# A new order for 1680 operations: linear attention fused with a squared-ReLU FFN on one core

## The chip, the core and the metric

The kernel runs on one core of a Trainium2 chip. Its engines are TensorE (PE, matmuls; PEld is its weight load), VectorE (DVE), ScalarE (ACT), GpSimd (POOL) and SyncE (SP); each works through its own instructions in order and waits on semaphores for the others. Matmuls write into PSUM, which has eight banks of 512 fp32 numbers in each of 128 partitions. The metric is the time of one execution in microseconds (us), as the median of several runs; a profile shows one execution.

## The reference

The input is q, k, v of 8 batches, 8 heads, 576 positions and 64 channels, a projection w_phi of 64 x 128, and the weights of an FFN. What is computed, cut to what matters:

```python
def phi(x):
    proj = np.einsum('bhsd,df->bhsf', x, w_phi)
    proj = proj - np.max(np.abs(proj), axis=-1, keepdims=True)
    return np.concatenate([np.exp(proj), np.exp(-proj)], axis=-1)
q_p, k_p = phi(q), phi(k)
kv  = np.einsum('bhsf,bhsd->bhfd', k_p, v)
z   = np.sum(k_p, axis=2)
num = np.einsum('bhsf,bhfd->bhsd', q_p, kv)
den = np.einsum('bhsf,bhf->bhs', q_p, z)[..., None] + 1e-06
x   = (num / den).transpose(0, 2, 1, 3).reshape(4608, 512)
h   = np.maximum(x @ w_in, 0.0)          # w_in: 512 x 2048
out = (h * h) @ w_out                    # w_out: 2048 x 512
```

The matmuls take bf16 operands; inputs and output are fp32.

## The kernel before, in words

The program first writes down a plan: 1680 operations, each with its engine, a function that issues its instructions, and the tags that it reads and writes. They are numbered in the order of writing, and the numbers are used as names below ("projection 42"). Then it issues them in the order of a table. Nothing decides at run time; each engine's instructions stand in exactly that order.

**Attention, by batch.** POOL loads k, q and v (L249, L257, L269, L278) into two buffers each. Of the first two batches PE transposes k and q (L320), and DVE or ACT copies the result to SBUF (kT, qT; L193 is the copy on DVE, L195 that on ACT). From batch 2 on SP does it with a DMA transpose (L331). A projection of k (Pk: L347, and in halves L379 for the first group) fills two banks; *three* operations then read it: the largest magnitude on DVE (mk, L405, in halves L386), and exp of plus and minus the projection on ACT (kp and kn, L411, in halves L394). The maximum isn't needed by the exps: its own exp (va, L420) is multiplied into v (L428) instead. PE sums kp and kn against v (L450, L462) and the result kv is copied to SBUF. For q the first batches use L491/L498 and turned projections Fq (L569, exps L584); from batch 3 on projections Pq with maxima L531 and exps qf (L544), which SP turns by DMA (qpn). NA (L648) and NB are the two parts of the numerator, with a DVE scaling SA (L660) between; then a reciprocal (L670) and xo, the quotient (L674), which closes the numerator's banks. There are three xo buffers. SP turns xo into xT by DMA (L708); for the first batch PE does it.

**FFN, by chunks of 512 tokens.** F1 (L788; L799, L813, L827 for the first chunk) multiplies four 128 x 512 blocks into one bank; relu moves it to hr, on ACT (L765) or on DVE (L767), and frees the bank; DVE squares it (L774). F2 (L882) sums sixteen blocks into one bank in four operations; a copy takes it to ot, and SP stores it. There are four hr and four ot buffers.

All the program between batches is one interleaved stream: while PE works on the FFN of one chunk, DVE and ACT prepare the next batch's attention.

**What sets the order.** Five tables at the end: ORDER (the order of issue), BASES (a bank for each use of PSUM), STATES (for operations that two engines can do, which does it), GATES (for each load of batches 2 to 7, the operation behind which POOL issues it) and FILL (dummy matmuls on a tile `warm` ahead of a PE operation, L961). PSUM is one tile, and what touches the same bank from two engines is kept in the order of the program by semaphores, readers too. POOL keeps at most eight loads outstanding. The lines which use the tables:

```python
    def arrange(self):
        for op in self.ops:
            if op.alt is not None and STATES[op.group] == "1":
                op.eng, op.occ, op.lat = op.alt
        for g, b in zip(self.banks, BASES):
            g.base = int(b)
        return [self.ops[i] for i in ORDER]
...
        if now[0].seq in GATES:
            dep(i, plan.ops[GATES[now[0].seq]].ins, mybir.DependencyClass.Sync)
...
    for op in plan.arrange():
        if op.seq in FILL:
...
            bank, n = FILL[op.seq]
            for _ in range(n):
                pin(nc.tensor.matmul(out=psum[:, bank, :P], lhsT=warm, rhs=warm, start=True, stop=True))
```

Of the kernel before, what the change touches and what calls it, by code (L numbers as in the profile page):

```python
# [108 lines left out]
def kernel(  # L109
# [945 lines left out]
)  # L1055
STATES = (
    '0100000001011000100001110011010100000000100011100100110000001010000000010110000100000000001000000100'
    '0100101101000000011010011011010000010100000111010001000100000000010110000100001101000000000000111111'
    '101000110110110110111110101110000'
)  # L1060
GATES = {
# [46 lines left out]
```

## Time and profile before

| | |
|---|---|
| median of 3 runs | 344.05 us (343.82 to 346.07) |
| span of the profiled execution | 344.8 us, 0.75 above the median |
| PE busy | 335.5 us, 97% of the span |
| DVE busy | 264.2 us, 77% |
| ACT busy | 225.4 us, 65% |
| POOL busy | 95.5 us, 28% |
| moved by DMA | 51.51 MB, 149 GB/s on average |

"Busy" is the time in which an engine executes; a matmul that waits for a semaphore isn't busy. The shares are means over stages of different kinds: a startup of some 26 us in which the first two batches are prepared and no FFN runs yet, a middle in which FFN and attention are interleaved, and a stretch from about 250 us in which only the FFN of the last chunks is left. Rows of groups give the number of instructions behind x, then busy time and mean nanoseconds of one, then the idle time ahead of them with what ended it. Rows of waits give the total, how often, and the longest.

### The profile page before, as it was taken

How to read it: one execution, taken by the hardware profiler on the slowest of the kernel's cores; microseconds unless marked ns; L12 is line 12 of the kernel's file. 1: busy time of each engine (PE TensorE's matmuls, PEld its weight loads, DVE VectorE, ACT ScalarE, POOL GpSimd, SP SyncE). 2: the span in 40 equal slices, each digit the busy share in tenths (PEclk: the TensorE clock that was granted, in tenths of full speed). 3: DMA queues.
4: the chain of work that ended last, by engine and by line, in shares of the span. 5: the costliest groups of instructions: out<-in, count | busy, mean ns of one | idle time of the engine just before them, and what ended most of it. 6: DMA issues, size and time to landing. Idle time of an engine off the chain costs nothing.

```text
span 344.8 us, 8417 instructions
## 1 busy us (share of the span) xinstructions
PE 335.5 (97%) x3389; PEld 188.3 (55%) x3389; DVE 264.2 (77%) x485; ACT 225.4 (65%) x393; POOL 95.5 (28%) x143
## 2 busy tenths in 40 slices
PE   8999999799999999999999999999999999999995
PEld 7679776444654555545545554565555444444443
DVE  4999999699877987788898999687876635757510
ACT  4999996489898898476887797798475503210031
POOL 8670671681730390104604051240000000000000
PEclk9999999999999999999999999999999999999999
DMA  9999999999999999999999999999864821101024
GB/s 139 179 206 202 199 132 157 153 118 205 170 175 172 227 165 185 195 182 183 171 207 172 199 164 195 188 154 168 196 125 96 157 62 38 63 0 61 32 68 115
DMA packets 142935, 51.51 MB, mean 149 GB/s; under 512 B 111472, under 2 KB 138416, under 8 KB 142896
## 3 DMA queue, kind: packets, MB, share of 16 engines
q1 hardware_dynamic: 97488, 32.35, 50.7%
q0 software_dynamic: 44960, 18.23, 46.7%
q8 instruction: 26, 0.43, 0.5%
q10 hardware_dynamic: 448, 0.39, 0.4%
q14 instruction: 13, 0.11, 0.1%
HBM read 36.73 MB, written 9.44 MB: 134 GB/s over the span
## 4 chain that ended last, share of the span: by engine, by line
PE 87%; DMA 6%; DVE 3%; ACT 1%; POOL 1%; issue 0%; POOLq 0%; DVEq 0%; SPq 0%
PE psum L788 32%; PE psum L882 31%; PE psum L648 5%; PE psum L462 5%; PE psum L347 5%; DMA xT<-xo 4%; DMA qpn<-qf 3%; PE psum L827 2%; PE psum L569 1%; DVE mk L405 1%; PE psum L813 1%; PE psum L799 1%; PE psum L846 1%; PE psum L450 1%; PE psum L320 1%; PE psum L961 1%
## 5 line engine op out<-in xcount | busy, mean ns | idle before, releaser
L882 PE MATMUL psum<-wout,h 128*128 128x512 bf16 x560 | 132.6, 380 | 0.0
L788 PE MATMUL psum<-xT,win 128*128 128x512 bf16 x448 | 106.1, 379 | 0.6 <-DMA xT<-xo 0.6
L765 ACT ACTIVATE hr<-psum 128x512 bf16<-128x512 f32 x98 | 57.1, 600 | 57.7 <-PE psum L788 50.2
L882 PEld LDWEIGHTS <-h 128*128 128x128 bf16 x560 | 51.1, 98 | 56.5 <-issue 0.3
L788 PEld LDWEIGHTS <-win 128*128 128x128 bf16 x512 | 46.7, 97 | 51.9 <-DMA xT<-xo 1.4
L774 DVE TENSOR_TENSOR h<-hr 128x512 bf16<-128x512 bf16 x144 | 56.0, 415 | 18.7 <-ACT hr L765 18.2
L544 ACT ACTIVATE qf<-psum 128x1024 bf16<-128x1024 f32 (+1 forms) x50 | 46.1, 939 | 5.5 <-PE psum L347 2.0
L405 DVE TENSOR_REDUCE mk<-psum 128x8 f32<-128x1024 f32 (+1 forms) x38 | 42.4, 1120 | 3.9 <-PE psum L347 2.0
L411 ACT ACTIVATE kn<-psum 128x1024 bf16<-128x1024 f32 (+1 forms) x38 | 35.7, 948 | 8.2 <-PE psum L347 4.7
L411 ACT ACTIVATE kp<-psum 128x1024 bf16<-128x1024 f32 (+1 forms) x38 | 35.8, 951 | 4.8 <-PE psum L347 4.0
L648 PEld LDWEIGHTS <-qpn 128*128 128x128 bf16 x624 | 27.5, 97 | 16.6 <-issue 3.1
L767 DVE TENSOR_SCALAR hr<-psum 128x512 bf16<-128x512 f32 x46 | 31.1, 684 | 5.7 <-PE psum L788 4.2
L660 DVE TENSOR_TENSOR psum<-psum,en 128x520 f32<-128x520 f32 (+1 forms) x39 | 27.2, 702 | 10.3 <-PE psum L648 6.1
L648 PE MATMUL psum<-kv,qpn 128*128 128x65 bf16 x624 | 30.6, 193 | 2.5 <-DVE xo L674 2.4
L269 POOL DMA_DIRECT2D xq<-in_q_dram x24 | 17.3, 727 | 55.2 <-DVE h L774 14.3
L531 DVE TENSOR_REDUCE mq<-psum 128x8 f32<-128x1024 f32 (+1 forms) x25 | 27.8, 1112 | 3.3 <-PE psum L347 2.5
L674 DVE TENSOR_TENSOR xo<-psum,rden 128x512 bf16<-128x512 f32 (+1 forms) x39 | 26.4, 684 | 3.7 <-DMA xT<-xo 3.2
L249 POOL DMA_DIRECT2D xk<-in_k_dram x27 | 20.0, 744 | 32.5 <-ACT en L508 16.0
L584 ACT ACTIVATE qpn<-psum 128x1024 bf16<-128x1024 f32 (+1 forms) x30 | 26.8, 955 | 2.5 <-PE psum L569 2.2
L195 ACT ACTIVATE ot<-psum 128x512 f32<-128x512 f32 x24 | 14.4, 598 | 20.3 <-PE psum L882 20.1
L428 DVE TENSOR_TENSOR va<-xv,va 128x1280 bf16<-128x1280 bf16 (+2 forms) x34 | 23.4, 714 | 0.8 <-ACT va L420 0.8
L249 POOL DMA_DIRECT2D xv<-in_v_dram x27 | 19.9, 744 | 14.7 <-PE psum L788 11.1
(79 smaller groups left out, 348.9 us busy)
## 6 DMA issues: line engine op xcount, KB each, us to landing
out_dram<-ot SPq DMA_DIRECT2D x32, 256.0 KB, 2.9
xk<-in_k_dram POOLq DMA_DIRECT2D x25, 128.0 KB, 5.6
xq<-in_q_dram POOLq DMA_DIRECT2D x24, 128.0 KB, 4.5
xv<-in_v_dram POOLq DMA_DIRECT2D x24, 128.0 KB, 5.0
win<-in_moe_w_in_dram POOLq DMA_DIRECT2D x4, 512.0 KB, 9.8
wout<-in_moe_w_out_dram POOLq DMA_DIRECT2D x4, 512.0 KB, 15.1
xq<-in_q_dram POOLq DMA_DIRECT2D x4, 256.0 KB, 6.4
out_dram<-ot SPq DMA_DIRECT2D x6, 128.0 KB, 2.3
```

Of the source, the lines that this page charges most:

```text
L249: pin(nc.gpsimd.dma_start(out=x[:, m0 + a * 512 : m0 + z * 512].rearrange("p (h x) -> p h x", x=4 * D), in_=src[b][2 * a : 2 * z, 0:512, : ...
L405: pin(nc.vector.tensor_reduce(out=mk_view(g), in_=ps2(pj)[:, :, : n * Fd].rearrange("p e (i f) -> p e i f", f=Fd), axis=AX.X, op=ALU.max, ...
L411: pin(nc.scalar.activation(out=dst[slot][:, :, :n, :].rearrange("p e i f -> p e (i f)"), in_=ps2(pj)[:, :, : n * Fd], func=ACT.Exp, scale= ...
L531: pin(nc.vector.tensor_reduce(out=mqb[:, c, :, :n], in_=ps2(pj)[:, :, : n * Fd].rearrange("p e (i f) -> p e i f", f=Fd), axis=AX.X, op=ALU ...
L544: pin(nc.scalar.activation(out=o, in_=i_, func=ACT.Exp, scale=sgn))
L648: pin(nc.tensor.matmul(out=o[:, u // 4, u % 4 * D1 : (u % 4 + 1) * D1], lhsT=qpn[slot][:, sg * half + u * m : sg * half + u * m + P], rhs= ...
L660: pin(nc.vector.tensor_tensor(out=o, in0=o, in1=enb[:m, c, :].rearrange("t (b h) -> t b h", b=2).to_broadcast([m, 2, 4, D1]), op=ALU.mult))
L765: pin(nc.scalar.activation(out=hr[sl], in_=ps1(g), func=ACT.Relu))
L767: pin(nc.vector.tensor_scalar(out=hr[sl], in0=ps1(g), scalar1=0.0, scalar2=None, op0=ALU.max))
L774: pin(nc.vector.tensor_tensor(out=dst, in0=i_, in1=i_, op=ALU.mult))
L788: pin(nc.tensor.matmul(out=o, lhsT=win[mc // 4][:, kc, mc % 4 * P : (mc % 4 + 1) * P], rhs=x, start=(kc == 0), stop=(kc == KC - 1)))
L882: pin(nc.tensor.matmul(out=ps1(g), lhsT=h2[c % 2][mc // 4][:, mc % 4, tt * P : (tt + 1) * P], rhs=wout[mc // 4][:, mc % 4, :], start=(mc = ...
```

## The change

All five tables get other contents; the 1680 operations, their functions and the data stay the same. The core of the diff:

```diff
 ORDER = [
-    2, 0, 1, 13, 14, 12, 8, 6, 7, 5, 3, 4, 11, 19, 40, 41, 9, 42, 46, 48, 10, 74, 66, 47, 75, 15, 67, 76, 45, 43, 18,
-    68, 44, 77, 17, 71, 58, 88, 16, 90, 59, 70, 89, 26, 91, 60, 27, 78, 69, 92, 20, 49, 80, 81, 79, 28, 50, 61, 51,
...
+    2, 1, 6, 5, 0, 13, 12, 11, 8, 14, 3, 7, 4, 40, 9, 41, 19, 42, 10, 48, 44, 47, 16, 74, 43, 66, 45, 75, 17, 46,
+    58, 67, 76, 59, 18, 79, 77, 15, 90, 88, 78, 91, 68, 26, 89, 69, 70, 60, 28, 92, 49, 80, 98, 21, 71, 93, 50, 27,
...
 BASES = (
-    '1451670476225101724453266476024460120674067172476254720032457624204004626222251065446606141516020635'
...
+    '0013767456235003614453246776024460220644067773557654621022547624204004626222250135406606141116020653'
...
 STATES = (
-    '0100000001011000100001110011010100000000100011100100110000001010000000010110000100000000001000000100'
...
+    '1000000000100100100011110010000100000010100000000101011100001000000101010000100100100100111100110100'
...
 GATES = {
-    355: 3, 356: 170, 357: 152, 358: 146, 359: 141, 360: 307, 361: 150, 362: 202, 363: 71, 364: 268, 365: 132,
...
+    355: 43, 356: 44, 357: 146, 358: 62, 359: 65, 360: 110, 361: 157, 362: 122, 363: 89, 364: 166, 365: 67,
...
 FILL = {
-    40: (0, 26), 42: (0, 11), 74: (0, 5), 76: (0, 7), 58: (0, 10), 60: (4, 10), 92: (0, 7), 131: (0, 16),
-    156: (7, 2), 101: (7, 2), 128: (7, 9), 134: (5, 4), 142: (5, 6),
+    40: (0, 27), 42: (1, 4), 74: (2, 10), 58: (3, 7), 90: (6, 13), 60: (1, 5), 156: (0, 24), 128: (7, 21),
+    134: (2, 8), 119: (7, 3),
 }
```

In numbers: relus on ACT go from 98 to 92 and on DVE from 46 to 52; copies of F2 results on ACT from 24 to 22 and on DVE from 11 to 13; copies of kv on ACT from 16 to 19 and on DVE from 16 to 13. Of PE's operations the large sequence stays close to what it was, with neighbours exchanged: ahead of NA 297, for example, stand now the F2 operations 521 and 535, which followed it. In POOL's order three other loads of batch 2 (362, 363 and 369) come ahead of the last of its k pieces. The dummy matmuls are 122 instead of 115.

The first place is ACT at the start of the program, from the first exp on. kp0 and kn0 are the exps of the first projection (42: two halves, operations 46 and 47 of one and 44 and 45 of the other), kn3, kp3, kn4, kp4 those of projections 68 and 76. Before:

```order
L394 ACTIVATE kp0_84<-psum_61 128x512 [waits PE_49]
L394 ACTIVATE kn0_90<-psum_61 128x512
L394 ACTIVATE kn0_90<-psum_61 128x512 [waits DVE_49]
L394 ACTIVATE kp0_84<-psum_61 128x512
L411 ACTIVATE kn3_93<-psum_61 128x1024 [waits DVE_49,PE_49]
L411 ACTIVATE kp3_87<-psum_61 128x1024
L411 ACTIVATE kp4_88<-psum_61 128x1024 [waits DVE_49]
```

And now:

```order
L394 ACTIVATE kp0_84<-psum_61 128x512 [waits DVE_49]
L394 ACTIVATE kn0_90<-psum_61 128x512 x2
L394 ACTIVATE kp0_84<-psum_61 128x512 [waits DVE_49]
L411 ACTIVATE kn4_94<-psum_61 128x1024 [waits PE_49]
L411 ACTIVATE kp4_88<-psum_61 128x1024 [waits DVE_49]
L411 ACTIVATE kp3_87<-psum_61 128x1024 [waits DVE_49]
```

The first exp waits now for DVE instead of PE, since DVE reads that half first; behind the four exps stand those of projection 76 and 68, with a wait for DVE before kp4, kp3 and kn2 each.

The second place is DVE in the same stretch. mk0 are the maxima (128x4 the halves of projection 42, then whole ones, 128x2x4), kT0 and qT0 copies of transposes. Before:

```order
L386 TENSOR_REDUCE mk0_100<-psum_61 128x4 [waits PE_49]
L193 COPY kT0_80<-psum_61 128x512 [waits PE_49] x2
L386 TENSOR_REDUCE mk0_100<-psum_61 128x4 [waits Activation_49]
L405 TENSOR_REDUCE mk0_100<-psum_61 128x2x4 [waits PE_49]
L193 COPY kT0_80<-psum_61 128x512 [waits PE_49]
L193 COPY qT0_82<-psum_61 128x512 [waits PE_49,Activation_49]
L193 COPY qT0_82<-psum_61 128x512 [waits PE_49]
L405 TENSOR_REDUCE mk0_100<-psum_61 128x2x4 [waits Activation_49]
```

And now:

```order
L386 TENSOR_REDUCE mk0_100<-psum_61 128x4 [waits PE_49]
L386 TENSOR_REDUCE mk0_100<-psum_61 128x4 [waits Activation_49]
L193 COPY kT0_80<-psum_61 128x512 [waits PE_49] x3
L405 TENSOR_REDUCE mk0_100<-psum_61 128x2x4 [waits Activation_49]
L193 COPY qT0_82<-psum_61 128x512 [waits PE_49] x2
L405 TENSOR_REDUCE mk0_100<-psum_61 128x2x4 [waits PE_49]
L193 COPY qT0_82<-psum_61 128x512 [waits PE_49]
```

The two half maxima, between which two copies stood, are neighbours now, and the second waits for ACT at once; the whole maxima that follow wait for ACT (kn4) and PE.

The third place is ACT in batch 4, where kp2 and kn2 (128x2x256) are the exps of projection 757 and kn5, kp5 those of projection 769; hr are relus of F1. Before:

```order
L411 ACTIVATE kn2_92<-psum_61 128x2x256 [waits DVE_49]
L411 ACTIVATE kp2_86<-psum_61 128x2x256
L411 ACTIVATE kn5_95<-psum_61 128x1024 [waits PE_49]
L765 ACTIVATE hr3_127<-psum_61 128x512 [waits DVE_49,PE_49]
L765 ACTIVATE hr2_126<-psum_61 128x512 [waits PE_49]
L514 ACTIVATE en1_105<-mq1_103 64x2x2
L508 ACTIVATE en1_105<-mq1_103 128x8
L514 ACTIVATE en1_105<-mq1_103 64x2x2
L411 ACTIVATE kp5_89<-psum_61 128x1024 [waits DVE_49]
```

And now:

```order
L411 ACTIVATE kp2_86<-psum_61 128x2x256 [waits PE_49]
L411 ACTIVATE kn2_92<-psum_61 128x2x256 [waits DVE_49]
L765 ACTIVATE hr3_127<-psum_61 128x512 [waits Activation_49]
L411 ACTIVATE kn5_95<-psum_61 128x1024 [waits PE_49]
L411 ACTIVATE kp5_89<-psum_61 128x1024
L765 ACTIVATE hr2_126<-psum_61 128x512 [waits DVE_49,PE_49]
```

Two relus, which stood between kn5 and kp5, now have one ahead of kn5 and one behind kp5. The last of these rows frees the bank of F1 709, which F1 727 uses again after NB 624 and F2 877; before, F1 727 used another bank.

More of the change, by code (lines that the diff above doesn't have):

```diff
@@ L967 @@
 ORDER = [
[81 rows of a table removed]
[82 rows of a table added]
 ]
 BASES = (
-    '1451670476225101724453266476024460120674067172476254720032457624204004626222251065446606141516020635'
-    '4220064626464240250445055510434165452020406007260606265547757461450712416435202000140262662264254104'
-    '1551457035140012622661654044422220716767000171574407664050016672456222446545465760614001372764624645'
-    '01402666226250104515244025230334655275421561732601266761410402454666250351330'
+    '0013767456235003614453246776024460220644067773557654621022547624204004626222250135406606141116020653'
+    '4220064626464240200445151505413055260020401707260606205507504465043742116425202060423262663164434041'
+    '1535503024141120622630544044224221713662061371627607666050510672406222626546516706474600471114524641'
+    '40214566211300251510714043625173436170071275506342026761317402454666250351330'
 )
 STATES = (
-    '0100000001011000100001110011010100000000100011100100110000001010000000010110000100000000001000000100'
-    '0100101101000000011010011011010000010100000111010001000100000000010110000100001101000000000000111111'
-    '101000110110110110111110101110000'
+    '1000000000100100100011110010000100000010100000000101011100001000000101010000100100100100111100110100'
+    '0000110100000000100101001100000010001000001000001110010000010001011110010001101100001011100011010011'
+    '100010110010110110111110101110000'
 )
 GATES = {
[11 rows of a table removed]
[11 rows of a table added]
 }
 FILL = {
-    40: (0, 26), 42: (0, 11), 74: (0, 5), 76: (0, 7), 58: (0, 10), 60: (4, 10), 92: (0, 7), 131: (0, 16),
-    156: (7, 2), 101: (7, 2), 128: (7, 9), 134: (5, 4), 142: (5, 6),
+    40: (0, 27), 42: (1, 4), 74: (2, 10), 58: (3, 7), 90: (6, 13), 60: (1, 5), 156: (0, 24), 128: (7, 21),
+    134: (2, 8), 119: (7, 3),
 }
```

179 rows, old and new, of tables (GATES, ORDER) are left out of this document.

## The prediction

> **What bounds the kernel now.** I read first the page's shares of the span, then the windows, then what TensorE (PE) waited for.
>
> ```profile
> PE 335.5 (97%) x3389; PEld 188.3 (55%) x3389; DVE 264.2 (77%) x485; ACT 225.4 (65%) x393; POOL 95.5 (28%) x143
> ...
> PEclk9999999999999999999999999999999999999999
> ...
> L882 PE MATMUL psum<-wout,h 128*128 128x512 bf16 x560 | 132.6, 380 | 0.0
> L788 PE MATMUL psum<-xT,win 128*128 128x512 bf16 x448 | 106.1, 379 | 0.6 <-DMA xT<-xo 0.6
> ```
>
> PE is busy for 97% of the span at an undisturbed clock, and the two FFN groups alone hold 238.7 us. The same matmuls are issued after the change, so only the remaining 3% and the dummies can shrink; what can grow is anything for which PE has to wait.
>
> ```profile
> 6.15:24.50 18.35, 17.26 (x305) 13.62 (x304) 18.35 (x35) 18.12 (x38) 13.73 (x20) 1.00 1.52 190
> 60.00:70.00 10.00, 7.63 (x82) 4.35 (x80) 6.74 (x12) 4.57 (x6) 6.81 (x11) 1.00 1.34 157
> 100.00:150.00 50.00, 49.28 (x524) 26.16 (x522) 41.88 (x69) 38.57 (x69) 12.90 (x19) 1.00 1.26 186
> 150.00:200.00 50.00, 50.00 (x516) 26.58 (x515) 43.56 (x81) 39.47 (x70) 14.20 (x21) 1.00 1.22 185
> ```
>
> In these windows the columns after the stretch and its length are the busy time of PE, of the weight loads, of DVE, ACT and POOL. They show two regimes. From 6.15 to 24.5 us DVE is busy for 18.35 of 18.35 us and ACT for 18.12: **the startup is bound by DVE and ACT**, and what PE does there is largely dummies. Later PE is full, and DVE and ACT have 10 to 25% to spare.
>
> ```profile
> PE psum L648 <- DVE xo L674: 2.4, 1, 2.4
> ...
> PE psum L788 <- DMA xT<-xo: 0.6, 1, 0.6
> ```
>
> After the startup PE waits in only two places worth a name: once for 2.4 us on the first numerator NA and once for 0.6 us on an F1.
>
> **The startup: +3.2.** The rows around the first projections, of all engines in order of time:
>
> ```profile
> 4.53 1.22 PE L961 MATMUL psum<-warm 128*128 128x128 bf16 x11
> 4.78 0.42 DVE L193 COPY kT<-psum 128x512 bf16<-128x512 bf16 x1 [0.59 <-PE psum L320]
> 5.68 0.40 PE L379 MATMUL psum<-wphi,kT 64*128 64x128 bf16 x8
> 6.11 0.60 ACT L394 ACTIVATE kp<-psum 128x512 bf16<-128x512 f32 x1 [2.10 <-PE psum L379]
> 6.15 0.69 DVE L386 TENSOR_REDUCE mk<-psum 128x4 f32<-128x512 f32 x1 [0.94 <-PE psum L379]
> 6.61 1.08 ACT L394 ACTIVATE kn<-psum 128x512 bf16<-128x512 f32 x2
> 6.75 0.75 DVE L193 COPY kT<-psum 128x512 bf16<-128x512 bf16 x2
> 7.42 0.68 DVE L386 TENSOR_REDUCE mk<-psum 128x4 f32<-128x512 f32 x1
> 8.01 1.22 DVE L405 TENSOR_REDUCE mk<-psum 128x8 f32<-128x1024 f32 x1
> 8.04 1.06 ACT L411 ACTIVATE kn<-psum 128x1024 bf16<-128x1024 f32 x1
> 8.94 1.07 ACT L411 ACTIVATE kp<-psum 128x1024 bf16<-128x1024 f32 x1
> 9.14 0.42 DVE L193 COPY kT<-psum 128x512 bf16<-128x512 bf16 x1
> ...
> 18.67 0.42 DVE L193 COPY kT<-psum 128x512 bf16<-128x512 bf16 x1
> ...
> 26.73 0.96 PE L813 MATMUL psum<-xT,win 128*128 128x128 bf16 x14
> ```
>
> From starts of neighbours I take what one operation holds its engine: a half maximum 0.60 (6.15 to 6.75), a half exp 0.50, a full maximum 1.13 (8.01 to 9.14), a full exp 0.90 (8.04 to 8.94), a copy 0.33. Before, while ACT reads one half of projection 42, DVE reads the other and then copies; DVE never stands still until 18.67, where the second batch begins.
>
> The three readers of a projection carry waits on each other, although none needs another's data. That these waits are paid shows in the rows by form:
>
> ```profile
> L405 DVE TENSOR_REDUCE mk<-psum 128x8 f32<-128x1024 f32 x31 | 37.6, 1218 | 2.3 <-ACT kp L411 1.0 <-PE psum L347 0.6 <-ACT kn L411 0.4
> L411 ACT ACTIVATE kn<-psum 128x1024 bf16<-128x1024 f32 x31 | 31.6, 1026 | 4.8 <-PE psum L347 3.9 <-DVE mk L405 0.8
> L411 ACT ACTIVATE kp<-psum 128x1024 bf16<-128x1024 f32 x31 | 31.6, 1031 | 1.6 <-PE psum L347 1.2 <-DVE mk L405 0.2
> L411 ACT ACTIVATE kn<-psum 128x512 bf16<-128x512 f32 x7 | 4.2, 598 | 3.5 <-DVE mk L405 2.7 <-PE psum L347 0.8
> L411 ACT ACTIVATE kp<-psum 128x512 bf16<-128x512 f32 x7 | 4.2, 598 | 3.2 <-PE psum L347 2.8 <-DVE mk L405 0.4
> ```
>
> An exp waits for the maximum (0.8, 0.2, 2.7, 0.4) and the maximum for an exp (1.0, 0.4): 5.5 us in all, and the reason can only be the bank. The Trainium skill, PSUM — Partial Sum Buffer, section "PSUM bank collisions raise a hardware error", says the same and speaks against the new order: two engines may not touch one bank at once, two reads included, so software has to put one behind the other. By that rule, with which these rows agree, the sum comes out as below; if only a write against a read had to be kept apart, it would be that of the first rival.
>
> Now the new order, with these holds. Fewer dummies stand ahead of projection 42, so it starts right behind its copy (4.78 + 0.42), at 5.25 instead of 5.68: -0.45. Maximum 48 runs 5.7 to 6.4. ACT's first exp (44) wants the half that 48 reads and starts at 6.45; then 47 at 6.95, which ends at 7.5; maximum 43 wants 47's half, so DVE stands idle from 6.3 to 7.5: **+1.2**. Then 43 and three copies, to 9.15. Projection 76 ends at 9.1; exp 79 takes it from 9.1 to 10.1, and only then may maximum 77 start: **+1.0**. Next ACT waits for 77, for 69 and for 61 in turn, and its half exps come late, so that half maximum 52 waits for exp 56: **+0.5**. Last, maximum 157 comes behind projection 156, ahead of which 24 dummies now stand instead of 2, and product V (83) waits for factors from ACT: **+0.7**. One copy (97) goes from ACT to DVE: **+0.2**. The sum is 1.2 + 1.0 + 0.5 + 0.7 + 0.2 - 0.45 = 3.15, say **+3.2 us** at the copy of 18.67 and so at the first FFN matmul of 26.73, since DVE has no gap in which to catch up. Bounds: 1.5 if only the first two waits and half of the others are real less the earlier start, 4.5 if the dummies collide too.
>
> **The two waits of PE: -3.0.** The second stage:
>
> ```profile
> 64.75 0.69 DVE L674 TENSOR_TENSOR xo<-psum,rden 128x512 bf16<-128x512 f32 x1 [3.17 <-DMA xT<-xo]
> 65.36 0.68 DVE L405 TENSOR_REDUCE mk<-psum 128x4 f32<-128x512 f32 x1
> 65.50 0.40 PE L648 MATMUL psum<-kv,qpn 128*128 128x65 bf16 x8 [2.37 <-DVE xo L674]
> 66.08 0.60 ACT L411 ACTIVATE kn<-psum 128x512 bf16<-128x512 f32 x1 [2.31 <-DVE mk L405]
> ```
>
> NA 297 needs the bank that xo 292 frees, and 292 needs its xo buffer, which a DMA transpose is still reading until 64.66: SP issues that transpose behind the k transposes of batch 2, and these wait for loads. This chain hangs on DMA and stays where it is, or comes 0.6 later because three more loads stand ahead of batch 2's k pieces. PE comes to it later: by 3.2 us of startup, and by two F2 of 0.86 each that now go ahead of 297. Cover of 4.9 us against 2.4 + 0.6: the wait goes. The F1's 0.6 goes likewise (fewer transposes are queued ahead on SP). So both rows, 2.4 + 0.6 = **-3.0**. If transposes move with the startup, the F2s alone save 1.7 - 0.6 = 1.1, which is the bound at the other end. All other loads and transposes have by their gates at least as much lead over their users as before; I put them at nothing, covered by the loads' place in POOL's queue; if that cover is gone one late batch costs what 297 cost, 2.4.
>
> **The body: +3.9.** PE runs at 0.216 us for each 512-column matmul, and ACT frees most FFN banks:
>
> ```profile
> 139.56 5.18 PE psum L882 x24
> ```
>
> ```profile
> L765 ACT ACTIVATE hr<-psum 128x512 bf16<-128x512 f32 x98 | 57.1, 600 | 57.7 <-PE psum L788 50.2 <-DVE h L774 4.8 <-PE psum L347 0.7
> L767 DVE TENSOR_SCALAR hr<-psum 128x512 bf16<-128x512 f32 x46 | 31.1, 684 | 5.7 <-PE psum L788 4.2 <-ACT hr L765 0.7
> ```
>
> 5.18 / 24 = 0.216, so one F1 holds PE for 0.86. Going through both orders with this, I counted how long after an F1's end its bank is written again: under 1.2 us in 5 cases before (all freed by ACT), in 16 after (4 of them freed by DVE). A relu needs 0.60 on ACT and 0.68 on DVE, so about 0.35 to 0.5 us are left for whatever stands ahead of it. The place in batch 4 that the order rows above show: from the end of projection 757, ACT runs half exp kp (0.5), waits for the half maximum on DVE (0.6), half exp kn (0.5), a relu (0.5), exps kn and kp (0.9 each), and then the relu of F1 709 (0.6), 4.7 us with the hand-overs, some 0.05 each. PE needs 4.2 for what stands between, and then wants the same bank for F1 727: it waits 0.5. An exp met halfway costs 0.45 less the slack, hence near 0.1 to 0.2; between that and 0.5 I take 0.35, nearer the worked place, for each of the 11 cases that are new: **+3.9**. Bounds: 0 (the five cases of before cost nothing in PE's waits) and 6.
>
> Relus that change engine move 6 of 0.68 us to DVE; in windows where it has over 12% spare this is free. Dummies grow from 115 to 122, inside PE's startup waits. The order at the end is the same: nothing.
>
> **Sum.** 344.8 + 3.2 - 3.0 + 3.9 = 348.9 for the profiled span; the median of the runs, 344.05, lies 0.75 under the span of before, so 348.9 - 0.75 = **348.1**.
>
> **The rivals.**
> 1. *The waits between readers stay covered* (faster). DVE and ACT find work in between, the startup gives -0.45 + 0.2, the F2s save 1.1 at 297, the F1's 0.6 goes, the body costs nothing: 344.8 - 0.25 - 1.1 - 0.6 - 0.75 = 342.1. For it: of 19.5 us of such waits that the old order could have (worked out under 3) only 5.5 were seen. Against it: 18.35 of 18.35 us leave nothing to find in the startup. It decides if DVE's idle time before 20 us stays under 1 us.
> 2. *Only the startup is paid, and the DMA waits swallow it*: 344.8 + 3.2 - 3.0 - 0.75 = 344.25. For it: DVE at 43.56 and ACT at 39.47 of 50 us have room, and PE had no wait on a relu.
> 3. *The waits between readers fill the spare time of both engines.* Taking for each adjacent pair of readers on two engines the first's hold less the other engine's work placed between, the order gives 19.5 us before and 58.9 after; of the 19.5, 5.5 were seen, 28%. Of the 39.4 more, 28% are 11, of which the startup has some 3; if PE pays the other 8: 344.8 + 3.2 - 3.0 + 8 - 0.75 = 352.3. For it: the holds of a projection's readers are 1.13 + 0.90 + 0.90, longer than any slack of a bank. Against it: two engines share it, and half falls where PE has other work.
>
> **Chances.** Forecast (347 to 350.5) 0.46; rival 1 0.13; rival 2 0.27; rival 3 0.12; that the waits don't appear in the compiled order at all is excluded by its rows, and 0.02 is left for other things. The range reaches from rival 1 to a little above rival 3: 342.5 (1.5 of startup, -3.0, no body: 342.55) to 353.5. One per cent, about what a measurement here can tell from no change, is 340.6 to 347.5. Under it lies only rival 1's tail, 0.05; inside lie its rest, rival 2 and the forecast's lower edge, 0.41; above it 0.54.
>
> **What would show it.** The first FFN matmul (L813) at about 30 instead of 26.73, and DVE under 16 of 18.35 us in the startup window; mk waiting for kp or kn and they for mk by over 12 us in all instead of 5.5; no PE wait on xo at 65; new PE waits on hr, a few tenths each, from 70 to 230 us. The forecast is wrong if the first FFN matmul comes before 28, if PE still waits over 1 us for xo, or if PE's waits on hr stay under 1 us or pass 6.

## The result, and the profile after

The changed kernel takes **378.3 us** (375.5 to 380.4) against 344.2 us of the kernel before on the same chips: a ratio of 1.096, 95% interval 1.092 to 1.100. It is slower, as forecast, but by 34 us where 4 were forecast, and the time lies far above the range. The profiled execution spans 373.8 us, 29.0 more than that of before. Every run takes 1.7 to 1.9 us longer than its own span, so the profiled execution of before was some 2 us longer than its median run, and that of after some 3 us shorter; that is why the spans differ by less than the times.

The six runs of the changed kernel follow the clock that was granted to TensorE: 375.5 us at 0.995, 377.6 at 0.991, 378.3 to 378.6 at 0.986, 380.4 at 0.982. The runs of the kernel before lie at 0.994 to 1.000. From this an estimate: 378 x (1 - 0.986) = 5 of the 34 us went by the lower clock.

From the page after: the busy shares, the granted clock and the chain that ended last, and behind them the chain of before for comparison.

```profile
PE 341.6 (91%) x3396; PEld 191.3 (51%) x3396; DVE 271.0 (73%) x490; ACT 223.5 (60%) x388; POOL 95.6 (26%) x143
...
PEclk9999999999999999999989999999999999999999
...
PE 65%; ACT 16%; DVE 14%; issue 4%; ACTq 0%; DVEq 0%
```

```profile
PE 87%; DMA 6%; DVE 3%; ACT 1%; POOL 1%; issue 0%; POOLq 0%; DVEq 0%; SPq 0%
```

No engine has much more to do: PE is busy for 6 us more, DVE for 7 more, ACT for 2 less. What grew is the time in which PE stands still, from 9.3 us of the span (344.8 - 335.5) to 32.2 (373.8 - 341.6). The chain of work that sets the end ran through ACT and DVE for 4% of the span before and does so for 30% now. What they wait for on that way stands in the waits of DVE and of ACT in the kernel after, where total, number and longest are given:

```profile
DVE mk L405 <- ACT kp L411: 10.9, 12, 2.0
DVE mq L531 <- ACT qf L544: 5.7, 7, 1.8
DVE mk L405 <- ACT kn L411: 5.6, 7, 1.6
DVE mk L386 <- ACT kn L394: 1.5, 2, 1.2
```

```profile
ACT qf L544 <- DVE mq L531: 14.5, 15, 2.1
ACT kp L411 <- DVE mk L405: 10.6, 10, 1.3
ACT kn L411 <- DVE mk L405: 7.5, 10, 1.3
ACT kp L394 <- DVE mk L386: 2.8, 2, 2.6
```

These are the waits of readers of one projection for each other: 23.7 us on DVE and 35.4 on ACT, 59.1 in all. In the profile of before the same pairs make 6.9: the rows of kp, kn and mk that the prediction shows, and for q

```profile
ACT qf L544 <- DVE mq L531: 0.8, 2, 0.4
DVE mq L531 <- ACT qf L544: 0.7, 2, 0.5
```

None of these waits hands data over. What reaches PE of them in the kernel after is spread widely:

```profile
PE psum L347 <- ACT kp L411: 3.6, 4, 1.8
PE psum L648 <- DVE psum L660: 2.6, 2, 2.1
PE psum L788 <- ACT kn L411: 2.4, 3, 1.2
PE psum L347 <- ACT qf L544: 2.4, 4, 1.4
PE psum L648 <- ACT kp L411: 2.1, 3, 1.0
PE psum L788 <- ACT qf L544: 2.0, 2, 1.2
PE psum L882 <- ACT kn L411: 2.0, 1, 2.0
...
PE psum L788 <- ACT hr L765: 0.5, 1, 0.5
```

A projection, an F1, an F2 and a numerator wait for an exp (kp, kn, qf), which still holds the bank that they are to write; only 0.5 us go to a relu. One such chain, around 188 us in the kernel after:

```profile
187.48 1.02 ACT L411 ACTIVATE kp<-psum 128x1024 bf16<-128x1024 f32 x1
188.38 1.03 ACT L544 ACTIVATE qf<-psum 128x1024 bf16<-128x1024 f32 x1
188.53 1.23 DVE L405 TENSOR_REDUCE mk<-psum 128x8 f32<-128x1024 f32 x1 [2.00 <-ACT kp L411]
189.67 0.70 DVE L660 TENSOR_TENSOR psum<-psum,en 128x520 f32<-128x520 f32 x1
189.79 1.02 ACT L411 ACTIVATE kn<-psum 128x1024 bf16<-128x1024 f32 x1 [0.37 <-DVE mk L405]
190.42 0.55 PE L648 MATMUL psum<-kv,qpn 128*128 128x65 bf16 x8 [2.12 <-DVE psum L660]
```

DVE stands still for 2.00 us until kp is through with the projection's bank, then takes its maximum, and only then the scaling for which PE has been waiting: 2.12 us. The scaling itself had nothing to do with kp; it merely stood behind a maximum that stood between two exps.

### The profile page after: what moved, and what is told of

Its sections match the earlier page's. It is cut to its first block, busy times and chain, and to the rows that moved or that the text cites. A ratio compares the mean times of both kernels' runs of the same rounds, so it can differ in the third digit from the quotient of the medians.

```text
span 373.8 us, 8409 instructions
## 1 busy us (share of the span) xinstructions
PE 341.6 (91%) x3396; PEld 191.3 (51%) x3396; DVE 271.0 (73%) x490; ACT 223.5 (60%) x388; POOL 95.6 (26%) x143
## 4 chain that ended last, share of the span: by engine, by line
PE 65%; ACT 16%; DVE 14%; issue 4%; ACTq 0%; DVEq 0%
PE psum L788 24%; PE psum L882 23%; DVE mk L405 5%; PE psum L648 5%; ACT qf L544 5%; ACT kp L411 4%; DVE mq L531 4%; ACT kn L411 4%; PE psum L347 4%; PE psum L462 2%; PE psum L827 1%; ACT qpn L584 1%; PE psum L799 1%; PE psum L813 1%; PE psum L961 1%
## 5 line engine op out<-in xcount | busy, mean ns | idle before, releaser
L765 ACT ACTIVATE hr<-psum 128x512 bf16<-128x512 f32 x92 | 53.2, 600 | 48.7 <-PE psum L788 38.1
L544 ACT ACTIVATE qf<-psum 128x1024 bf16<-128x1024 f32 (+1 forms) x50 | 45.9, 935 | 19.0 <-DVE mq L531 14.5
L405 DVE TENSOR_REDUCE mk<-psum 128x8 f32<-128x1024 f32 (+1 forms) x38 | 42.5, 1123 | 17.8 <-ACT kp L411 10.9
L767 DVE TENSOR_SCALAR hr<-psum 128x512 bf16<-128x512 f32 x52 | 35.1, 683 | 5.9 <-PE psum L788 5.5
L195 ACT ACTIVATE ot<-psum 128x512 f32<-128x512 f32 x22 | 13.0, 594 | 36.4 <-PE psum L882 36.3
L249 POOL DMA_DIRECT2D xv<-in_v_dram x27 | 20.1, 753 | 42.4 <-ACT en L514 20.3
L584 ACT ACTIVATE qpn<-psum 128x1024 bf16<-128x1024 f32 (+1 forms) x30 | 27.2, 950 | 4.0 <-PE psum L569 3.3
L674 DVE TENSOR_TENSOR xo<-psum,rden 128x512 bf16<-128x512 f32 (+1 forms) x39 | 26.7, 686 | 0.8
```

The costliest lines, as they stand in the source:

```text
L249: pin(nc.gpsimd.dma_start(out=x[:, m0 + a * 512 : m0 + z * 512].rearrange("p (h x) -> p h x", x=4 * D), in_=src[b][2 * a : 2 * z, 0:512, : ...
L405: pin(nc.vector.tensor_reduce(out=mk_view(g), in_=ps2(pj)[:, :, : n * Fd].rearrange("p e (i f) -> p e i f", f=Fd), axis=AX.X, op=ALU.max, ...
L544: pin(nc.scalar.activation(out=o, in_=i_, func=ACT.Exp, scale=sgn))
L584: pin(nc.scalar.activation(out=o, in_=i_, func=ACT.Exp, scale=sgn))
L765: pin(nc.scalar.activation(out=hr[sl], in_=ps1(g), func=ACT.Relu))
L767: pin(nc.vector.tensor_scalar(out=hr[sl], in0=ps1(g), scalar1=0.0, scalar2=None, op0=ALU.max))
```

## The experiments

The names below: theory A, the readers of one projection hold each other up, and this costs the time; theory B, the tighter reuse of banks; theory C, loads, transposes and the choice of engines. A group is a projection with its two exps on ACT and its maximum on DVE; there are 67.

**The maxima without the bank, after (a_sbmax).** Each maximum that shares its projection with ACT reads a small SBUF tile of zeros instead, in as many elements, and still waits for the projection:

```diff
-                    out=mk_view(g), in_=ps2(pj)[:, :, : n * Fd].rearrange("p e (i f) -> p e i f", f=Fd),
+                    out=mk_view(g), in_=fk[:, :, :n].to_broadcast([P, 2, n, Fd]),
...
+        if now[0].seq in MAXOF:
+            dep(i, plan.ops[MAXOF[now[0].seq]].ins, mybir.DependencyClass.Sync)
```

> The kernel after, with one thing taken away: the maxima of projections that ACT reads too (mk, and mq from batch 3 on) read a small SBUF tile of zeros with the same number of elements, so DVE has the same work in the same order, still behind the same projection, but shares no bank with ACT's exps. Left out: the true maxima. Theory A, the readers of one projection hold each other up: the waits of kp, kn and qf for mk and mq and the other way round (about 55 us summed over both engines in the profile of after) vanish, and with them nearly all of the loss: 341 to 349 us. Theory B, the tighter reuse of banks: still 368 or more. Theory C, loads, transposes and the engine choice: still 370 or more.

Measured: 353.9 us, ratio 1.029 (1.024 to 1.033). So 24 of the 34 us went with one shared resource, while DVE's work stayed what it was, by the group of these maxima:

```profile
L408 DVE TENSOR_REDUCE mk<-fk 128x8 f32<-128x1024 f32 (+1 forms) x38 | 42.1, 1112 | 2.0 <-PE psum L350 1.8
```

The same 38 maxima hold 42.5 us in the kernel after. B and C are refuted as the main cause. (The edit also keeps a maximum from holding a bank that PE wants next; but the waits of PE in the kernel after show none for a maximum, except 0.2 us of a weight load.) Yet the time is 5 us above what A gave, and its PE waits show why: the transposes behind it.

```profile
PE psum L791 <- ACT qf L547: 3.7, 1, 3.7
PE psum L651 <- DVE xo L677: 2.0, 1, 2.0
```

```profile
ACT qf L547 <- DMA qpn<-qf: 7.6, 5, 4.5
DVE xo L677 <- DMA xT<-xo: 3.1, 1, 3.1
```

In the last two rows, ACT's qf waits for a transpose that still reads its buffer, and DVE's xo for another. In the kernel after the first was 0.6 and the second absent, presumably because PE came late.

**The same edit, before (b_sbmax).** The control.

> The control: the kernel before with the same edit (the maxima read an SBUF tile of zeros; the true maxima are left out). Theory A: before had only 5.5 us of these waits, under cover, so 342 to 345 us, no more than 1 per cent faster. If this kernel became much faster, say under 335 us, the edit itself would make DVE's work cheaper and the run of after with it would not tell A from the rest.

Measured: 344.8 us, ratio 1.001 (0.998 to 1.004). The edit itself is worth nothing.

**Only which reader goes first, after (a_readers).** In 20 groups the maximum changes its place among the exps in ORDER, for example

```diff
-    58, 67, 76, 59, 18, 79, 77, 15, 90, 88, 78, 91, 68, 26, 89, 69, 70, 60, 28, 92, 49, 80, 98, 21, 71, 93, 50, 27,
+    58, 67, 76, 59, 18, 77, 79, 15, 90, 88, 78, 91, 68, 26, 89, 69, 70, 60, 28, 92, 49, 80, 98, 21, 71, 93, 50, 27,
```

where maximum 77 now stands ahead of exp 79; DVE's and ACT's own sequences don't change.

> The kernel after, with only the order among readers changed: for 20 projections whose maximum stood between the two exps in the program's order (and one where it stood ahead), it now stands ahead of both or behind both. Every engine keeps its own sequence of instructions, the banks, the engine choice, the loads and the dummies stay; only which semaphore waits for which changes. Theory A: following the holds from row to row gives an estimate of 12 us less than after, 363 to 368 us. Theories B and C: no change, 376 to 380 us.

Measured: 364.2 us, ratio 1.056 (1.052 to 1.059): 14 us for a permutation that no engine notices in its own instructions. The waits between readers fell from 59.1 to 39.0 us; the two largest left are

```profile
ACT kn L411 <- DVE mk L405: 11.0, 9, 4.2
ACT qf L544 <- DVE mq L531: 8.7, 10, 1.9
```

**The same in the other direction, before (b_readers).** One part of the change alone, put into the old order:

```diff
-    2, 0, 1, 13, 14, 12, 8, 6, 7, 5, 3, 4, 11, 19, 40, 41, 9, 42, 46, 48, 10, 74, 66, 47, 75, 15, 67, 76, 45, 43, 18,
+    ... 42, 46, 48, 10, 74, 66, 75, 15, 67, 76, 43, 47, 45, 18, ...
```

> The kernel before, with one part of the change alone: for 27 of the 67 projections with readers on both engines the maximum takes, in the program's order, the place among the exps that it has in after (17 of them to between the two exps). Each engine's own sequence, banks, engine choice, loads and dummies stay those of before. Theory A: the waits between readers alone make it slower; following the holds from row to row gives an estimate of 385 us, so 375 to 395. If something that only comes together with after's other tables made the loss (B, C), 344 to 348 us.

Measured: 395.7 us, ratio 1.145 (1.139 to 1.151). The old banks, loads, engines and sequences, and 51 us lost, 17 more than by the whole change. Some 8 of them lie in the startup: the first FFN matmul starts at 34.8 us instead of 26.7, with the granted clock at 0.50 from 17 to 27 us. Its waits between readers come to 78.9 us:

```profile
DVE mq L531 <- ACT qf L544: 24.2, 10, 3.5
DVE mk L405 <- ACT kp L411: 16.5, 8, 3.1
```

Three pairs can be laid side by side. From before to after these waits grew by 52.2 us and the time by 34.1; from after to a_readers they fell by 20.1 and the time by 14.1; from before to b_readers they grew by 72.0 and the time by 50.8. In these three the time moves by 0.65 to 0.71 us for each us of waits summed over both engines. That is no constant: a_sbmax lost all 59.1 us of such waits and got 24.4 back, 0.41 for each, and a_reseq, below, lost 37.0 and got 14.0 back, 0.38. And these times hold the lower clock as well: b_readers ran at 0.965 to 0.974, an estimate of 10 to 14 of its 51 us (395 x 0.026 to 0.035).

Counted in ORDER, the maximum stands between the two exps in 17 of the 67 groups before, in 32 after, in 13 of a_readers and in 27 of b_readers. So a_readers has fewer of them than before and still 39.0 us of waits: the place among the exps alone doesn't tell the cost.

**Other banks, after (a_banks).** 109 uses of a bank get another number:

```diff
-    '0013767456235003614453246776024460220644067773557654621022547624204004626222250135406606141116020653'
+    '6730762416630130614543247766024460020644067773553654620022547624204004626222250135456606141116020635'
```

> The kernel after, with other PSUM banks only: 109 of the 377 uses of a bank get another number, so that banks are used again later; order, engines, loads and dummies are those of after. Theory A: the banks are a small part, 2 to 4 us less, 373 to 377 us. Theory B: most of the 29 us returns, 350 to 360 us. Theory C: no change.

Measured: 379.6 us, ratio 1.099 (1.094 to 1.104), the time of after, so the 2 to 4 us that A gave didn't come either. The profile shows two halves: the first FFN matmul starts at 33.6 us instead of 30.0, since the dummies wait for banks that are now in use (3.4 us) and the granted clock falls to 0.50 from 14.5 to 21.3 us; the rest is 2 us shorter. These banks don't give the loss back, as B had it; how much banks alone are worth was muddled by the startup.

**Engine choice, before (b_states).** STATES of after in the kernel before, nothing else.

> The kernel before with the engine choice of after alone (81 operations on the other engine: relus, copies of kv, transposes and outputs); order, banks, loads and dummies of before. Following the holds gives an estimate of 352 us, 8 more than before, since the order was written for the other choice; theory C (engine choice as the main cause of the 34 us) would need 360 or more; if it is free, 344 to 346.

Measured: 354.5 us, ratio 1.031 (1.027 to 1.034). It isn't free: an order that was written for one choice loses 10 us by another. That doesn't make it a 10 us part of the 34, because after has its own order for it; but part of what a_sbmax leaves may lie here.

**Old loads and transposes in the new order (a_sbmax_dma).** ORDER with POOL's and SP's operations in the sequence of before, GATES of before, and the maxima from SBUF.

```diff
 GATES = {
-    355: 43, 356: 44, 357: 146,
+    355: 3, 356: 170, 357: 152,
```

> The kernel after with the maxima read from SBUF as in a_sbmax (the true maxima are left out) and, on top, POOL's loads, their gates and SP's transposes and stores in the order of before. a_sbmax still was at 353.9 us: PE waited 3.7 us for an F1 behind an exp that waited for a transpose of qf, and the clock was granted at a half for some us behind that. If the order of loads and transposes makes this rest (theory C for the rest), the wait of 3.7 us goes and the time is 345 to 349 us; if the rest is in the order of PE, DVE and ACT, it stays at 351 to 356 us.

Measured: 371.3 us, ratio 1.075 (1.070 to 1.080), 17 us more than a_sbmax; both theories missed. The wait for transposes got longer instead of going away:

```profile
ACT qf L547 <- DMA qpn<-qf: 25.0, 8, 5.4
```

The new sequence of loads and transposes suits the new order of the engines better than the old one does. That rules out the old loads as a repair, and no more: which part of the new order makes the rest of a_sbmax stays open.

**The startup's readers alone, after (a_start).** Three of a_readers' 20 groups: maximum 43 ahead of exp 47 and 77 ahead of 79, both in the startup, and 203 ahead of 205 in batch 1. The first of them:

```diff
-    2, 1, 6, 5, 0, 13, 12, 11, 8, 14, 3, 7, 4, 40, 9, 41, 19, 42, 10, 48, 44, 47, 16, 74, 43, 66, 45, 75, 17, 46,
+    2, 1, 6, 5, 0, 13, 12, 11, 8, 14, 3, 7, 4, 40, 9, 41, 19, 42, 10, 48, 44, 16, 74, 43, 47, 66, 45, 75, 17, 46,
```

> The kernel after, with the place of the maximum among the exps changed for the projections of the first two batches alone (43 and 77 now ahead of the exps that stood before them); each engine's own sequence and all else as in after. Theory A for the startup: DVE's first two gaps (1.2 and 1.0 us by the prediction) go in part, the first FFN matmul comes about 2 us sooner than in after, and the whole is 2 us faster than after, about 376. If the startup's delay came from the dummies or the loads: no change.

Measured: 374.3 us, ratio 1.088 (1.085 to 1.091). By the ratio some 3 us better, but part of this is the clock: at 0.995 three of its runs took 373.9 to 374.4 us against 375.5 of after, and at 0.986 one took 376.6 against 378.3 to 378.6, so 1 to 2 us at the same clock. In the profile the first FFN matmul starts at 29.80, only 0.18 sooner, and the span, 374.8, isn't shorter. DVE's early gaps did close (maximum 43 follows 48 at once), and smaller ones opened elsewhere:

```profile
9.40 1.02 ACT L411 ACTIVATE kn<-psum 128x1024 bf16<-128x1024 f32 x1 [0.81 <-DVE mk L405]
...
12.16 0.42 DVE L193 COPY qT<-psum 128x512 bf16<-128x512 bf16 x1 [0.83 <-PE psum L320]
```

Still, DVE was ahead by then: the first maximum of q (L498) starts at 13.83 us, 1.13 sooner than in after. The next step lost most of this. From 13.3 to 16.7 us the granted clock was 0.50, which it never was in the startup of after; the 24 dummies ahead of projection 156 took 2.70 us instead of 1.50, and DVE waited 1.12 us for that projection instead of 0.36. So the run doesn't tell what the two groups alone are worth; a_sbmax, with all of them free, had its first FFN matmul at 27.2.

**A new sequence for all (a_reseq).** DVE's, ACT's and PE's operations moved by mostly up to five places on their engine, at the most 22, so that readers seldom meet; nothing is left out.

> The kernel after, with banks, engine choice, loads, transposes, stores and dummies unchanged, but DVE's, ACT's and PE's operations moved by up to some ten places each until, by the holds of the rows, readers of one projection hardly wait for each other. Theory A: nearly all of the loss returns without leaving any work out, estimate 344 us, so 343 to 353 us. Theories B and C: 368 us or more.

Measured: 364.3 us, ratio 1.054 (1.049 to 1.060): a miss for A's number, no better than the permutation. Waits between readers are down to 22.1 us, but other things took their place: the first FFN matmul starts at 33.0, behind two falls of the granted clock to 0.50 (from 7.8 and from 18.0 us), and

```profile
ACT qf L544 <- DMA qpn<-qf: 11.0, 5, 4.1
```

**The same search from the kernel before (b_reseq)**, to beat both.

> The kernel before, with DVE's, ACT's and PE's operations moved in the same manner, to find work for the wait of 2.4 us at 63 us and to shorten the startup. Estimate 342 us; by more than 1 us faster than before if the wait at 63 us was the only thing that held PE there, the same within 1 us if the next transpose takes its place.

Measured: 351.8 us, ratio 1.017 (1.014 to 1.021). Slower by 1.7%, and the profile shows losses like those of a_reseq: the first FFN matmul at 29.8, behind a clock of 0.50 from 19 to 22 us, and a PE wait on a transpose of qf of 1.9. No version was found that beats the kernel before.

**The two F2s, before (b_f2s).**

```diff
-    517, 377, 291, 292, 744, 382, 531, 376, 293, 367, 381, 297, 521, 370, 298, 378, 369, 380, 535, 552, 299, 351,
+    517, 377, 291, 292, 744, 382, 531, 376, 293, 367, 381, 521, 535, 297, 370, 298, 378, 369, 380, 552, 299, 351,
```

> The kernel before with only the two F2 operations 521 and 535 moved ahead of NA 297, as they stand in after. By the prediction's term they cover 1.7 of the 2.4 us for which PE waits there: 342.6 us, 0.3 to 0.5 per cent faster. If they are only missed behind it (NA's scaling on DVE then has no cover), the time stays within 0.5 us of before or rises by up to 1.5.

Measured: 345.7 us, ratio 1.004 (1.003 to 1.006): 0.4% slower, not faster. In its profile the wait of 2.4 us ahead of NA is gone, but two others have come, of NA for the scaling and of a projection for a maximum:

```profile
65.94 0.40 PE L648 MATMUL psum<-kv,qpn 128*128 128x65 bf16 x8 [0.79 <-DVE psum L660]
...
67.07 0.40 PE L347 MATMUL psum<-wphi,kT 64*128 64x128 bf16 x8 [0.39 <-DVE mk L405]
```

Half of the gain is given back at once. The span of this execution, 343.4, can't be set against the 344.8 of before, whose profiled execution was some 2 us longer than its median run; where the other half goes, no trace shows.

**Dummies in a wait (a_sbmax_warm).** In several of the runs above the granted clock fell behind waits of PE. From a_sbmax, windows of 4 us (busy time of PE, PEld, DVE, ACT, POOL, then the clock):

```profile
64.00:68.00 4.00, 1.99 (x30) 1.12 (x27) 1.63 (x2) 1.15 (x2) 4.00 (x7) 1.00 1.31 152
68.00:72.00 4.00, 4.00 (x22) 1.81 (x19) 3.71 (x6) 2.42 (x3) 3.63 (x6) 0.58 1.65 204
```

PE stands still for 2 us and then runs 4 us at a mean clock of 0.58; by windows of 1 us it is 0.50 for 3.4 us. The edit:

```diff
 FILL = {
+    297: (6, 32),
```

> a_sbmax (the true maxima are left out) with 32 dummy matmuls, 1.8 us of them, ahead of NA 297, where PE stood still for 2.0 us at 65 us and the clock of the 4 us from 68 on was granted at 0.58. If standing still is what lowers the clock, it stays at 1.00 from 66 to 76 us in the profile and the kernel gains about 1.7 us: 351.5 to 353. If the lower clock comes for another reason, the window shows 0.5 to 0.7 again and the time is that of a_sbmax, 354, or somewhat more.

Measured: 352.9 us, ratio 1.026 (1.022 to 1.029), 1 us less than a_sbmax, with intervals that overlap. At this place the profile agrees with the first reading:

```profile
68.00:72.00 4.00, 4.00 (x54) 2.17 (x50) 4.00 (x6) 2.76 (x4) 3.06 (x5) 1.00 1.36 188
```

The wait of 3.7 us at 152 us was also absent from this execution, so the profile's shorter span, 350.1, isn't due to the dummies alone. And at another place the clock fell here too, to 0.50 for 3.4 us from 113.5 us on, behind two waits of PE of 0.95 and 0.93 us with 0.6 us of work between them.

## Why the prediction was wrong, step by step

**The startup, +3.2: right in its size.** The first FFN matmul starts at 29.98 instead of 26.73, 3.25 later, and the gaps stand where they were foretold. DVE and ACT of the kernel after in order of time, then PE:

```profile
5.77 0.69 DVE L386 TENSOR_REDUCE mk<-psum 128x4 f32<-128x512 f32 x1 [0.71 <-PE psum L379]
6.50 0.60 ACT L394 ACTIVATE kp<-psum 128x512 bf16<-128x512 f32 x1 [2.56 <-DVE mk L386]
...
7.62 0.69 DVE L386 TENSOR_REDUCE mk<-psum 128x4 f32<-128x512 f32 x1 [1.15 <-ACT kn L394]
...
10.19 1.22 DVE L405 TENSOR_REDUCE mk<-psum 128x8 f32<-128x1024 f32 x1 [0.89 <-ACT kn L411]
...
29.98 1.07 PE L813 MATMUL psum<-xT,win 128*128 128x128 bf16 x16
```

1.15 and 0.89 were forecast as 1.2 and 1.0. Of the 3.25, all but 0.5 went when the maxima left the banks (a_sbmax, 27.2). That each term of the sum is right isn't shown by this: closing the first two gaps, 2.2 us by the working, brought DVE 1.1 us by 14 us in a_start.

**The two waits of PE, -3.0: they went, but for a dull reason.** PE's waits for xo are 0.6 us ahead of numerators and 0.4 ahead of projections, none of them at 65 us, and that for xT has disappeared from the list. PE simply came late. The part of the step that laid 1.7 us of cover to the two F2s failed: b_f2s showed that what they cover ahead of NA they uncover behind it.

**The body, +3.9: wrong, and this is the whole miss.** The span grew by 29.0, the startup by 3.25: 25.7 are left for the body, where the working had 3.9 - 3.0 = 0.9. Of these 25.7, PE stood still for 19.7 more than before and was busy for 6.0 more. The worked place was right to the tenth:

```profile
135.78 0.62 ACT L411 ACTIVATE kp<-psum 128x512 bf16<-128x512 f32 x1
136.43 0.69 DVE L405 TENSOR_REDUCE mk<-psum 128x4 f32<-128x512 f32 x1 [0.34 <-ACT kp L411]
137.15 0.60 ACT L411 ACTIVATE kn<-psum 128x512 bf16<-128x512 f32 x1 [0.76 <-DVE mk L405]
...
140.61 1.02 PE L788 MATMUL psum<-xT,win 128*128 128x512 bf16 x4 [0.50 <-ACT hr L765]
```

F1 727 waited 0.50 for the relu, as worked out. But the step then multiplied this by 11 F1s whose banks come round early, and PE's waits on relus are 0.9 us in all (0.5 and 0.4), which the prediction itself had named as a sign that it is wrong. The banks that PE wanted and didn't get were the projections' own, and the work that came late was that behind the maxima and exps. The step chose the wrong victims: it asked which *relu* stands behind a held-up exp, not which matmul stands behind the exps themselves.

**From the span to the time, -0.75.** The working took the profiled execution of before for an ordinary one, but it was some 2 us long. That did no harm, since only differences are added to it.

**Rival 3: right in its mechanism, mis-sized in one factor.** The count from the order gave 58.9 us of waits between readers, and 59.1 were measured. That these are so near is luck in part, since the same count gave 19.5 for the old order, where 6.9 were measured. The working then took only 28% of the growth, because in the kernel before 5.5 of 19.5 had been seen (6.9 with the rows of q, 35%). That share was a property of the old order, and b_sbmax shows that even this share cost no time there. The new order paid as much as was counted; that this is so because both engines step through its groups in turns is the likely reason, not a tested one. Without the factor the growth is 39.4 by the working's own count; with 0.65 to 0.71 us of time for each it comes to some 26 to 28 us, but these rates were found only by the runs and don't test it. Its place was the body as much as the startup.

**The bank rule.** The rule of the Trainium skill (PSUM — Partial Sum Buffer, "PSUM bank collisions raise a hardware error"), that two reads of one bank by two engines need an order as well, was weighed in the right direction: a_sbmax and b_readers show what that order costs here.

**Rivals 1 and 2** assumed that DVE and ACT have room. They have, by their busy shares (73% and 60%), but room in sum isn't room at the place.

What stays open: the last 9.5 us, from 353.9 to 344.4. The profile of a_sbmax shows 5.7 us of waits of PE on two transposes against 3.0 before, and two stretches at a lower clock (its runs were granted 0.985 to 0.995, an estimate of 2 to 5 us); that these are the whole isn't shown. Engine choice and dummies weren't tried in the new order.

## What to carry to other kernels

Where several engines read one PSUM bank, the order among these readers is part of the schedule: put the reader of the one engine ahead of or behind both of the other's, and other work between, and count for each adjacent pair how much of the first's hold isn't covered. Here such a move in 20 of 67 groups gave back 14 of 34 us, while moving more of the order for this purpose cost time elsewhere (a_reseq, b_reseq). If the count triples, let the range reach to all of it: the share that an older order happened to pay doesn't carry over (6.9 of 19.5 before, 59.1 of 58.9 after). Busy shares don't show such a loss; the chain of work that ends last does, where two engines that were off it appear with a seventh of the span each.

## What the hardware showed that was not expected

A lower clock followed a wait of PE of only 2 us: 0.58 over 4 us in a_sbmax. In the kernel after it is the wait of 2.12 us at 188 us quoted above, with 0.66 behind it:

```profile
185.00:190.00 5.00, 3.01 (x21) 1.31 (x19) 3.00 (x5) 4.09 (x5) 3.49 (x6) 1.00 1.46 186
190.00:195.00 5.00, 4.58 (x41) 2.49 (x41) 2.75 (x5) 3.21 (x5) 0.00 (x0) 0.66 1.67 107
```

By windows of 1 us both falls are to 0.50 for 3.4 us, which costs an estimated 5 x 0.34 = 1.7 us each. In a_sbmax_warm such a fall came behind two waits of less than 1 us each. In the startup the clock fell to 0.50 in a_banks, a_start, a_reseq, b_reseq and, for 10 us, in b_readers, while before and after stayed at 1.00 there. In the kernel before, a longer wait, 2.37 us at 63 us, had nothing of the kind behind it: its clock from 60 to 70 us reads 1.00. The Trainium skill, TensorE: Matmul & The Clock Gate, section "What's actually happening", has the clock fall after an idle window of about 3.4 us that runs free of the kernel. The free-running window agrees with one wait counting and another not; that a fall came behind waits of 2 us, shorter than the window, differs from it, and here the measurement decides. That the wait is the cause rests on one execution, that of a_sbmax_warm, where dummies in the wait left the clock at 1.00; what makes one wait count and another not stays open.
